# One chunk's down projection by seven products in place of eight, its sums laid into VectorE's rests

## The chip, the cores and the metric

The kernel runs on one core of a Trainium2 chip. The metric is the device time of one execution in microseconds (us), and lower is better. The profile has the engines PE (TensorE's matmuls), PEld (its weight loads), DVE (VectorE), ACT (ScalarE), POOL (GpSimd) and SP (SyncE, here only the issuer of transfers).

## The reference

A transformer layer on 2048 rows of 1024 values in bfloat16: windowed attention with an output projection, then a feed-forward part without a nonlinearity.

```python
h  = x + attention(layernorm(x), wqkv) @ wo        # wqkv 1024x3072, wo 1024x1024
g  = layernorm(h) @ w_gate                         # 1024x3584
u  = layernorm(h) @ w_up                           # 1024x3584
h2 = h + (g * u) @ w_down                          # 3584x1024
```

## The kernel before

The rows go in four chunks (0 to 3) of 512. Chunks 0 and 1 have their gate, up and down projections one chunk at a time. Chunks 2 and 3 are handled together, as a pair: their gate/up stage ("paired stage") and their down projection already use the Winograd form of Strassen's scheme, which makes a product of 2 by 2 blocks from seven block products in place of eight and pays with sums of blocks. The instruction order on each engine is the order of the program, and ScalarE and VectorE run their instructions in turn. The kernel keeps all matmul results in eight PSUM banks of 128x512, which they share.

The part that the change replaces, between chunk 1's gate/up stage and the paired stage:

```python
    hT = ffn1(1, lnT2)                 # gate and up of chunk 1, 28 tiles of hidden values
    ...
    l2, hs2 = wo_ln2(2)                # output projection of chunk 2, statistics, normalized rows
    ...
    ffn2(1, 0, hT, hs)                 # chunk 1's down projection, left half of the columns
    bg.finish(atts[3])
    l3, hs3 = wo_ln2(3)                # output projection of chunk 3
    activation_sums(l2, l3)            # the pair's sums of activations
    load_pair(0)
    load_pair(1)
    ...
    ffn2(1, 1, hT, hs, {0: first_sums})   # right half; beside it GpSimd's sums of weights

    def ffn2(c, hf, hT, hs, between={}):
        acc = [psum.tile([128, 512], F32, tag="mm", ...) for t in range(4)]
        ... # 28 tiles of hidden values x 4 blocks of rows = 112 matmuls a half
                    nc.tensor.matmul(acc[t][:], lhsT=hT[f][:, bass.ts(t, 128)],
                                     rhs=wts["wd", c, hf, b][:, j, :], ...)
        ...
        for t in range(4):
            ffn2_store(c, t, hf, acc[t], hs)   # VectorE adds the residual, then stores
```

The first step of the paired stage (`t1` to `t4` are the activation's sums, `sw` the sums of weights, `x y v z` its banks):

```python
        for i in gu:
            xb[i] = bank("x", i)
            product(xb[i], wt[:, 0:4, i, 0:128], b11, True)
            yb[i] = bank("y", i)
            nc.scalar.copy(yb[i][:], xb[i][:])
        for i in gu:
            vb[i] = bank("v", i)
            product(vb[i], sw[:, i, 0], t1, True)
            ...
            product(yb[i], sw[:, i, 1], t2, False)
            zb[i] = bank("z", i)
```

## Time and profile before

| | before |
|---|---|
| device time, median of 3 | 785.4 us (785.29 to 785.52) |
| TensorE busy | 99% |
| VectorE, ScalarE, GpSimd busy | 74%, 51%, 19% |
| end of chunk 1's gate/up to the paired stage (449.52 to 525.93) | 76.41 us |
| start of the paired stage to the end (525.93 to 785.8) | 259.9 us |

The last two rows are read off TensorE's timeline: the first matmul of chunk 2's output projection that follows the last one of chunk 1's gate/up stage, and the first `px` matmul. The stretch between them, which I call "the stage" below, begins here:

```profile
449.52 13.98 PE L507 MATMUL wo<-w_wo,oT 128*128 128x512 bf16 x63
```

It has 354 matmuls (the windows view counts 354 weight loads in it). TensorE is the bound, so the stage is read as so many matmuls at 0.216 us (112 of them took from 501.76 to 525.93) plus waits of TensorE; the busy time of the other engines matters only where one of them makes TensorE wait.

### The profile page before, as it was taken

What the parts mean: (1) busy time and instruction counts of PE and PEld (TensorE: products, weight loads), DVE (VectorE), ACT (ScalarE), POOL (GpSimd) and SP (SyncE); (2) the same over time, 40 slices, a digit from 0 to 9 for tenths busy, and PEclk for the clock granted to TensorE, in tenths of its full rate; (3) what the DMA queues carried; (4) which work ended last, traced back from release to release, by engine and by line L of the source; (5) the groups of instructions that cost most, each with busy time, mean ns of one, the idle gap of its engine ahead of it and who ended that gap; (6) DMA issues with size and microseconds to landing.
All of it is one profiled execution on the core that took longest, in us unless ns stands there. A gap on an engine that the chain in (4) does not pass through costs nothing.

```text
span 785.8 us, 10287 instructions
## 1 busy us (share of the span) xinstructions
PE 774.1 (99%) x3670; PEld 359.2 (46%) x3732; DVE 583.6 (74%) x727; ACT 402.9 (51%) x919; POOL 150.9 (19%) x160
## 2 busy tenths in 40 slices
PE   8999999999999999999999999999999999999998
PEld 6544444444444444444444444444444444444444
DVE  5619999999899998999979971733443444579862
ACT  3626534323476652965656610116677777749240
POOL 0000000010000200002000020058678687600000
PEclk9999999999999999999999999999999999999999
DMA  7999594895965878867556489433332423730001
GB/s 248 269 197 243 150 286 98 244 311 127 337 203 170 260 243 234 277 197 264 198 161 208 139 202 328 101 100 102 107 90 72 108 62 100 257 118 28 1 27 54
DMA packets 183683, 135.94 MB, mean 173 GB/s; under 512 B 79056, under 2 KB 176464, under 8 KB 181584
## 3 DMA queue, kind: packets, MB, share of 16 engines
q1 hardware_dynamic: 180048, 113.27, 51.0%
q0 software_dynamic: 3584, 22.02, 8.1%
q8 instruction: 29, 0.48, 0.3%
q14 instruction: 22, 0.18, 0.1%
HBM read 106.95 MB, written 22.02 MB: 164 GB/s over the span
## 4 chain that ended last, share of the span: by engine, by line
PE 74%; DVE 20%; issue 2%; SPq 1%; DMA 1%; ACT 0%; DVEq 0%
PE pu L386 12%; PE acc L605 12%; PE pg L386 12%; PE pz L658 6%; PE py L658 6%; PE px L658 6%; PE wo L507 5%; DVE prod L426 4%; PE ps L386 3%; PE pv L658 3%; PE dx L837 3%; PE dy L837 3%; DVE pv L469 2%; DVE prod L428 2%; SPq L223 1%
## 5 line engine op out<-in xcount | busy, mean ns | idle before, releaser
L386 PE MATMUL ps<-lnT,w_qkv 128*128 128x512 bf16 x721 | 159.0, 379 | 0.8
L386 PEld LDWEIGHTS <-w_qkv 128*128 128x128 bf16 x736 | 71.9, 98 | 86.0 <-issue 0.3
L386 PE MATMUL pu<-lnT,w_wu 128*128 128x512 bf16 x438 | 105.1, 379 | 0.6
L386 PE MATMUL pg<-lnT,w_wg 128*128 128x512 bf16 x440 | 105.1, 379 | 0.4
L605 PE MATMUL acc<-w_wd,gs 128*128 128x512 bf16 x438 | 96.7, 379 | 0.5
L300 ACT CAST sg<-ps 128x512 bf16<-128x512 f32 x96 | 54.8, 590 | 52.7 <-PE ps L386 48.9
L469 DVE TENSOR_TENSOR pv<-vD,at 128x4096 bf16<-128x4096 bf16 x32 | 72.5, 2286 | 0.3
L426 DVE TENSOR_TENSOR prod<-qD,kD 128x4096 bf16<-128x4096 bf16 x32 | 72.4, 2284 | 0.1
L658 PEld LDWEIGHTS <-sw 128*128 128x128 f16 x448 | 43.8, 98 | 52.9
L386 PEld LDWEIGHTS <-w_wg 128*128 128x128 bf16 x448 | 43.8, 98 | 52.8
L605 PEld LDWEIGHTS <-gs 128*128 128x128 bf16 x448 | 43.8, 98 | 52.9
L386 PEld LDWEIGHTS <-w_wu 128*128 128x128 bf16 x448 | 43.8, 98 | 52.9
L179 ACT ACTIVATE rs<-mv,eps 128x1 f32<-128x1 f32 x32 | 9.5, 297 | 101.2 <-DVE mv L176 98.2
L585 ACT CAST us<-pu 128x512 bf16<-128x512 f32 x56 | 33.1, 591 | 50.4 <-PE pu L386 49.3
L507 PE MATMUL wo<-w_wo,oT 128*128 128x512 bf16 x251 | 55.6, 379 | 0.3
L658 PE MATMUL px<-lnT,ws 128*128 128x512 bf16 x211 | 52.6, 379 | 0.6
L658 PEld LDWEIGHTS <-ws 128*128 128x128 f16 x336 | 32.9, 98 | 39.6
L481 POOL DMA_DIRECT2D od<-oD x4 | 2.2, 544 | 249.3 <-DVE oD L479 162.5
L637 POOL TENSOR_TENSOR sw<-ws 128x512 f16<-128x512 f16 x28 | 32.3, 1154 | 87.8 <-PE acc L605 47.2
L580 ACT CAST gs<-pg 128x512 bf16<-128x512 f32 x56 | 33.1, 591 | 12.8 <-PE pg L386 8.7
L507 PEld LDWEIGHTS <-oT 128*128 128x128 bf16 x256 | 25.0, 98 | 30.2
L428 DVE TENSOR_TENSOR prod<-prod 128x4096 bf16<-128x4096 bf16 x16 | 36.6, 2288 | 0.3
(244 smaller groups left out, 1196.6 us busy)
## 6 DMA issues: line engine op xcount, KB each, us to landing
w_wg<-in_B_w_gate_dram SPq DMA_DIRECT2D x14, 1024.0 KB, 6.7
w_wu<-in_B_w_up_dram SPq DMA_DIRECT2D x14, 1024.0 KB, 5.6
w_wd<-in_B_w_down_dram SPq DMA_DIRECT2D x16, 896.0 KB, 8.1
w_wo<-in_A_wo_dram SPq DMA_DIRECT2D x8, 1024.0 KB, 7.4
w_pair<-in_B_w_gate_dram SPq DMA_DIRECT2D x14, 512.0 KB, 4.0
w_pair<-in_B_w_up_dram SPq DMA_DIRECT2D x14, 512.0 KB, 5.3
w_qkv<-in_A_wqkv_dram SPq DMA_DIRECT2D x5, 1024.0 KB, 9.7
kd<-sg SPq DMA_DIRECT2D x32, 144.0 KB, 2.8
```

The costliest lines, as they stand in the source:

```text
L300: nc.scalar.copy(sg[:, HB:HB + TC], ps[:])
L386: nc.tensor.matmul(ps[:], lhsT=wt[:, ko, bass.ts(j, 128)], rhs=rhs[:, ko, :], start=(ko == 0), stop=(ko == KO - 1))
L426: nc.vector.tensor_tensor(prod[:, j], qD[:], kD[:, :, o:o + SUB], ALU.mult)
L428: nc.vector.tensor_tensor(prod[:, :, 0:16], prod[:, :, 0:16], prod[:, :, 16:32], ALU.add)
L469: nc.vector.tensor_tensor(pv[:, j], vD[:, :, o:o + SUB], at[:, w, None, :].to_broadcast((128, DH, SUB)), ALU.mult)
L507: nc.tensor.matmul(ps[:], lhsT=oTs[c][:, kk, t, :], rhs=wts["wo", c, hf][:, kk, :], start=(kk == 0), stop=(kk == KO - 1))
L580: nc.scalar.copy(gs[:], pg[:])
L585: nc.scalar.copy(us[:], pu[:])
L605: nc.tensor.matmul(acc[t][:], lhsT=hT[f][:, bass.ts(t, 128)], rhs=wts["wd", c, hf, b][:, j, :], start=(f == 0), stop=(f == NF - 1))
L637: nc.gpsimd.tensor_tensor(sw[:, i, 0], a21, a22, ALU.add)
L658: nc.tensor.matmul(ps[:], lhsT=lhs[:, ko, :], rhs=rhs[:, ko, :], start=(fresh and ko == 0), stop=(ko == 3), skip_group_check=not fresh)
L837: nc.tensor.matmul(ps[:, bass.ds(lo, n)], lhsT=lhs[k][:, bass.ts(q, 128)], rhs=rhs[k][:, bass.ds(lo, n)], start=(fresh and k == 0), stop=( ...
```

## The change

Chunk 1's down projection also goes by seven products. By the numbers that the prediction uses, TensorE has them in the order 1, 2, (output projection of chunk 3 after) 5, then 7, 6, 8, 9; product 1 stands ahead of chunk 2's output projection, products 2 and 5 between the two output projections, the others behind the second. Each has 28 matmuls. VectorE has to make four groups of sums of hidden values (S1 to S4, 14 sums of 256 columns each) and four sums of weights (T1 to T4), ScalarE and VectorE scale hidden values and weights from bfloat16 to float16, and the author has laid these sums between VectorE's adds of the two output projections. Beside that, a conversion of the tail moves from VectorE to ScalarE, the first sums of weights of the paired stage move from GpSimd to VectorE, the statistics of chunk 2 move from VectorE to ScalarE, one of the stage's two scale matmuls moves forward into chunk 1's gate/up stage, while one for chunk 1's hidden values comes in, and two more warming matmuls stand at the start. Cut to its core:

```diff
-    hT = ffn1(1, lnT2)
-    l2, hs2 = wo_ln2(2)
-    ffn2(1, 0, hT, hs)
-    l3, hs3 = wo_ln2(3)
-    ffn2(1, 1, hT, hs, {0: first_sums})
+    for q in range(2):
+        dprod(ex[q], q, E1["11"], fcells(dn["11"]), True)              # product 1
+    wo_adds(2, {1: scales, 2: ..., 6: lambda: t1_half(1), 7: lambda: s1(0, 10)})
+    s1(10, 14)
+    for q in range(2):
+        dprod(ex[q], q, E1["12"], fcells(dn["21"]), False)             # product 2
+        result(1, hs1[q], q, 0, ex[q], scale_d.inv, None)
...
+    for q in range(2):
+        dprod(ex[q], q, S1, fcells([dn["kx"], dn["vx"]]), True)        # product 5
+        nc.scalar.activation(p5t[:, q, :], ex[q][:], ACTF.Copy, scale=dn["inv"])
+    s3(0, 14)
+    wo_adds(3, {0: in_turn(lambda: s2(0, 7), lambda: ln_means(2)), 1: lambda: s2(7, 14),
+                2: in_turn(lambda: ln_devs(2), lambda: t2_half(0)), 3: lambda: t2_half(1), 4: lambda: t3_half(0),
+                5: in_turn(lambda: ln_act_rows(2, l2), lambda: t3_half(1)),
+                6: in_turn(lambda: ln_stats(3, 0), lambda: ln_stats(3, 1)), 7: lambda: ln_stats(3, 2)})
+    ln_stats(3, 3)                                                     # VectorE's statistics, ScalarE's root
+    for k in range(NP): ...                                            # S4, then T4
+    for q in range(2):
+        dprod(ey[q], q, EF["11"], fcells(dn["11"]), False)             # product 7
+        nc.scalar.copy(ex[q][:], ey[q][:])
+    scale_gu.total()
+    for q in range(2):
+        dprod(ex[q], q, EF["21"], fcells(dn["12"]), False)             # product 6
+        ...; result(1, hs1[2 + q], 2 + q, 1, ex[q], dn["inv"], et)
+    activation_sums(l2, l3, dn["px"])
+    weight_sums(0, nc.vector)
+    for q in range(2):
+        dprod(ex[q], q, EF["22"], fcells([dn["kx"], dn["vx"]]), False) # product 8
+        result(1, hs1[2 + q], 2 + q, 0, ex[q], dn["inv"], None)
+    for q in range(2):
+        dprod(ey[q], q, EF["12"], fcells(dn["22"]), False)             # product 9
+        result(1, hs1[q], q, 1, ey[q], dn["inv"], p5t[:, q, :])
...
-    conv_down(down["b21"])
+    conv_down(down["b21"], nc.scalar)
```

## The prediction

> **What bounds the kernel now.** I read the page's busy table first, then the waits of TensorE, then VectorE in order of time. The busy table:
>
> ```profile
> PE 774.1 (99%) x3670; PEld 359.2 (46%) x3732; DVE 583.6 (74%) x727; ACT 402.9 (51%) x919; POOL 150.9 (19%) x160
> ```
>
> TensorE is busy 99% of the span, so only fewer matmuls can pay, and every new wait of TensorE costs its full length. Busy matmuls can still be spaced out, so I looked at the issue rate. The timeline of TensorE:
>
> ```profile
> 501.76 24.34 PE L605 MATMUL acc<-w_wd,gs 128*128 128x512 bf16 x109
> 525.93 1.89 PE L658 MATMUL px<-lnT,ws 128*128 128x512 bf16 x8
> ```
>
> The second half of the down projection is 112 matmuls between 501.76 and 525.93, 0.216 us each (three records are missing). That is my unit. The waits of TensorE, and VectorE in order of time (start, us, group, idle before):
>
> ```profile
> PE dy L837 <- DVE dn_t2a L830: 1.0, 1, 1.0
> PE dy L837 <- DVE dn_t2b L830: 0.3, 1, 0.3
> ...
> 468.20 0.14 DVE L553 TENSOR_SCALAR ibd<-ebd 128x1 int32<-128x1 int32 x1
> 487.50 2.48 DVE L596 TENSOR_TENSOR h<-acc,h 128x512 bf16<-128x512 f32 x4 [19.16 <-PE acc L605]
> ...
> 525.48 2.48 DVE L596 TENSOR_TENSOR h<-acc,h 128x512 bf16<-128x512 f32 x4 [10.98 <-PE acc L605]
> ```
>
> In the part to be changed VectorE rests 19.16 us beside one half of the down projection and 10.98 us beside the other. These are the gaps in which the sums are to go. But they lie beside the very matmuls that the change cuts up, so the question is whether VectorE has each sum ready in time. The rows that I use (busy, mean ns):
>
> ```profile
> L830 DVE TENSOR_TENSOR dn_t2a<-dn_b22a,dn_t1a 128x3584 f16<-128x3584 f16 x1 | 2.0, 2007 | 0.0
> L876 DVE TENSOR_TENSOR dn_b11a<-hq,hq 128x512 f16<-128x512 f16 x6 | 2.1, 414 | 0.0
> L509 DVE TENSOR_TENSOR h<-wo,h 128x512 bf16<-128x512 f32 x32 | 21.4, 673 | 1.6 <-PE wo L507 1.6
> L784 ACT ACTIVATE dn_b22a<-dn_b22a,sbd 128x3584 f16<-128x3584 bf16 x1 | 3.3, 3283 | 0.0
> L784 ACT ACTIVATE hq<-hq,sbh 128x512 f16<-128x512 bf16 x12 | 7.6, 720 | 0.0
> ```
>
> [...]
>
> **Durations from start to start.** Sums of 3584: 1.93 (starts 730.75, 732.68, 734.62). Sums of 512: 0.334 (six in 2.08). The new sums are 256 wide, of which before has none: 0.52 ns an element between these two gives an estimate of 0.20. Scaling on VectorE: 1.07 for 3584, estimated 0.195 for 256. An add of the output projection 0.60; two statistics and their aggregate 1.44 (464.29 to 465.60, plus 0.13). VectorE starts 0.2 after a matmul group ends.
>
> **The change, part by part.**
>
> 1. Matmuls. Removed: 2 halves x 28 x 4 = 224. Added: 7 products x 2 banks x 14 = 196. Chunk 1's hidden values need their own scale: one more matmul. Net 27 x 0.216 = 5.8 us off TensorE. Without waits, from the end of chunk 1's gate/up stage to the first product of the paired stage would take 326 x 0.216 = 70.4 us in place of 76.2 (449.69 to 525.93).
>
> 2. Gate/up stage of chunk 1. ScalarE gets 28 absolute sums of 512, start to start 0.61; per pair of groups it then has 0.49 + 0.49 + 1.2 + 0.61 = 2.8 us in 3.46. It keeps up. VectorE gets two conversions (2.1 us) and is some 0.65 late from a later copy, so the last attention instruction ends at about 456 in place of 452.9. Nothing of this is on the path.
>
> 3. Output projection of chunk 2, TensorE 456.0 to 470.0 (with the one scale matmul), then product 2 to 476.0. VectorE waits for the third group (461.5) and from there is full: 6 adds 3.6, conversion of A22 2.7, of B12 2.1, T1 3.9, S1 14 x 0.20 = 2.8. Sum 15.1, so S1 is ready at 476.7; the result that frees the bank behind it takes 0.75. Product 5 starts at 477.5 in place of 476.0: **first wait 1.5 us**. It ends at 483.6.
>
> 4. Output projection of chunk 3, TensorE 483.6 to 497.4. VectorE begins with the first group's add at 485.5 and has 8 adds 4.8, S2 2.8, T2 and T3 4 x 1.93 = 7.7, four statistics 5.8, small ones 0.2: 21.3 us, to 506.9. The order list of the new kernel shows on ScalarE that the copy of product 7's banks (y to x) stands behind the four reciprocal roots of chunk 3, which need the last of these statistics. Root 0.6, copy 0.57: x is there at 508.1. TensorE has done product 7 and the other scale matmul at 503.7: **second wait 4.5 us**. Product 6 runs from 508.1 to 514.2.
>
> 5. VectorE from 506.9: the wait for the root 0.6, S4 2.8, T4 3.9, the scale chain 0.7, one add 0.7, the result of the first bank 0.75, so 516.6. Product 8 accumulates on this bank: **third wait 2.4 us**. Products 8 and 9 take 12.1, so the paired stage starts at about 528.8 in place of 525.93: 2.8 us later. Its own 12.1 us a step isn't touched; GpSimd's first sums (8 x 1.15) start at about 532 and end at 541, one step and a product later they are needed (542.6).
>
> 6. Tail. The conversion of B21 moves from VectorE (2.1) to ScalarE (6.4), which idles 7.51 us there. VectorE gets ahead by 2.1, but then one result waits for TensorE (1.1 of it lost). The waits of 1.0 and 0.3 shown above shrink by an estimated 0.75 together.
>
> 7. Start: two more warming matmuls end at 6.8, the first transpose now starts at 5.90. TensorE idles 1.03 for the weights at 7.7 and again at 9.85, which swallows the delay. I count 0.
>
> Sum: -5.8 + 1.5 + 4.5 + 2.4 + 0.2 (rounding) - 0.75 = +2.0, or 787.5.
>
> **Rivals.** (a) The order is right and TensorE never waits: 785.4 - 5.8 - 0.75 = 779. For it: the words of the change, and 37 us of rest on VectorE between 449.7 and 526. Against it: the count in 3 to 5, where each sum of durations exceeds the matmuls beside it; the rest beside chunk 0 and in the paired stage can't be used. (b) Half of it: sums of 256 are quicker than estimated or the copy reaches ScalarE earlier. If 0.05 less each, 56 sums give 2.8, but only 42 are on the path: 2.1 us, so 785.4. (c) Memory: chunk 3's attention output is fetched once chunk 2's projection is done (about 470 to 482; landing took up to 8.9 us from issue in before) for use at 483.6, and the converted B22 needs transfers issued after chunk 3's attention was stored at about 463. If they land 2 us late, 789.5. Against it: chunk 3's projection now uses chunk 2's weight blocks again, so 2 MB fewer are loaded here than before. (d) ScalarE becomes the bound in the gate/up stage by strict order: some us, 790. I give it little, 2.8 of 3.46 us is below full.
>
> **Range and chances.** My count says 787.5; the author has ordered the sums by need and will have looked at a trace, so (b) weighs more than (d). I say 786.8, with 781.5 (most of (a)) to 789.8 ((c)). For faster by 2% (769.7) more would have to go than the change removes: 1%. Slower by 2% (801) needs twice the waits that I count: 1%.
>
> **What would show it.** TensorE: 25 matmuls fewer in all (27 less, two warming ones more), and waits for VectorE ahead of product 5 (1.5), for the ScalarE copy ahead of product 6 (4.5) and for VectorE ahead of product 8 (2.4); VectorE without rest from the first add of chunk 3's projection to the statistics of its last rows; 256-wide sums at 0.27 us busy, 0.20 start to start. The step from gate/up to the paired stage should take 79 us. If it takes 71 to 74, my reading of the order or the durations of the sums are wrong; if it is right and the time isn't, the tail or the start moved.

The 0.195 us for a scaling of 256 follows from the trace of before like the 0.20 for a sum: 1.07 for 3584 and 0.263 for 512 (twelve from 706.67 to 709.82). The changed kernel has 0.196 (seven from 461.51 to 462.88).

## The result and the profile after

The changed kernel took 786.67 us (median of 4, 785.88 to 787.00), and the kernel before in the same rounds 785.46 us (785.29 to 785.55). A ratio is the mean time of one kernel's runs over that of the other's of the same rounds, so not quite the ratio of the medians; here it is 1.0014, with a 95% interval of 0.9997 to 1.0032: the same. 786.8 had been predicted.

The page of the changed kernel begins with its busy table; the columns are busy time, share of the span, number of instructions.

```profile
PE 768.9 (98%) x3648; PEld 355.4 (45%) x3707; DVE 614.6 (78%) x810; ACT 470.9 (60%) x1033; POOL 141.8 (18%) x152
```

Weight loads, of which there is one for every matmul and fewer records are missing (the down projection of chunks 0 and 1 before has 448 of them for its 448 matmuls, and 438 records of these), fell from 3732 to 3707: the 25 that were predicted. TensorE's work is 5.2 us less, VectorE's 31.0 us more, ScalarE's 68.0 us more. Where TensorE waits now (total, times, longest):

```profile
PE ex L784 <- ACT ex L963: 4.0, 1, 4.0
PE ex L784 <- DVE h L789: 2.0, 2, 1.3
...
PE dy L784 <- DVE h L789: 0.6, 1, 0.6
...
PE dy L784 <- DVE prodx L777: 0.3, 1, 0.3
```

The first two lines are new. They are the three waits of the stage (the profile counts a wait from the modelled end of the matmul before it, 0.379 us after its start, where the next one follows after 0.216 without a wait; from start to start each is 0.16 us longer: 1.48, 4.15 and 0.84); the last two are what is left of the tail's waits of 1.0, 0.6 and 0.3. The same in TensorE's timeline (start, length, group, and in brackets the wait before it and what ended it):

```profile
447.30 6.21 PE L784 MATMUL ex<-w_dn,gs 128*128 128x512 f16 x28
...
474.89 1.67 PE L784 MATMUL ex<-kx,es 128*128 128x512 f16 x7 [1.32 <-DVE h L789]
...
481.15 13.76 PE L829 MATMUL wo<-w_wo,oT 128*128 128x512 bf16 x62
...
505.16 2.09 PE L784 MATMUL ex<-w_dn,gs 128*128 128x512 f16 x7 [3.99 <-ACT ex L963]
507.05 2.98 PE L784 MATMUL ex<-prodx,gs 128*128 128x512 f16 x7
...
513.73 1.67 PE L784 MATMUL ex<-kx,gs 128*128 128x512 f16 x7 [0.68 <-DVE h L789]
...
525.81 1.89 PE L677 MATMUL px<-lnT,ws 128*128 128x512 bf16 x7
```

From top to bottom: product 1, product 5 with its wait, chunk 3's output projection, product 6 with its wait, product 8 with its wait, the paired stage. The stage takes 525.81 - 447.30 = 78.51 us. Seven matmuls of product 5 took 1.67 us in the record, seven of product 6 took 2.98: TensorE was slow there. The windows view says why (columns: window, its length, busy us of PE, PEld, DVE, ACT, POOL, the granted clock, DMA share, GB/s):

```profile
501.00:505.10 4.10, 0.17 (x1) 0.00 (x0) 3.44 (x10) 1.68 (x8) 0.00 (x0) 1.00 0.93 196
505.10:509.00 3.90, 3.84 (x12) 1.47 (x12) 3.90 (x14) 3.90 (x6) 0.00 (x0) 0.65 1.13 308
```

In the wait itself the granted clock is 1.00; in the 3.9 us behind it, 0.65. In half-microsecond windows the clock is at 0.50 from about 506.3 to 509.7, for 3.4 us. Product 6 takes 7.9 us (505.16 to 513.05) in place of the 6.2 that it takes at full clock (e4 below).

What held product 6 up, on VectorE and on ScalarE:

```profile
482.86 0.69 DVE L831 TENSOR_TENSOR h<-wo,h 128x512 bf16<-128x512 f32 x1 [4.54 <-PE wo L829]
...
503.85 0.21 DVE L182 BATCH_NORM_AGGREGATE mv<-st 128x2 f32<-128x12 f32 x1
504.66 0.16 DVE L954 SCALAR_TENSOR_TENSOR lnroom<-mv,rs 128x4 f32<-128x4 f32 x1 [0.60 <-ACT rs L186]
...
512.93 0.75 DVE L789 SCALAR_TENSOR_TENSOR h<-ex,inv_h1d,et 128x512 bf16<-128x512 f32 x1
```

```profile
504.10 0.29 ACT L185 ACTIVATE rs<-mv,eps 128x1 f32<-128x1 f32 x1 [0.86 <-DVE mv L182]
504.42 0.20 ACT L186 ACTIVATE rs<-rs 128x1 f32<-128x1 f32 x1
504.53 1.06 ACT L963 COPY ex<-ey 128x512 f32<-128x512 f32 x2
```

VectorE waits 4.54 us for chunk 3's first projection, then has no rest from 482.86 until its last statistics end at about 504.06. ScalarE makes the root of these, and only then the copy of product 7's bank, which was complete on TensorE since 501.0. The two copies take 1.06 us from 504.53; product 6 begins at 505.16, when the first of them is done. VectorE's result at 512.93 is the one that lets product 8 begin.

Two more measures. From the paired stage to the end it takes 784.8 - 525.81 = 259.0 us, 0.9 less than before. And the two profiled runs are not a fair pair: their spans are 785.8 before and 784.8 after, the other way round than the medians, because the profiled run of before had a late start, with its first 512-wide matmul at 19.38 us, against 17.08 after. Its granted clock is 0.94 in the first 30 us and at 0.50 from about 9.7 to 13.2, where that of after is 1.00. That is what the first experiment looks at.

### The profile page after: what moved, and what is told of

Read it like the earlier page. It is cut to its first block, busy times and chain, and to the rows that moved or that the text cites. A ratio compares the mean times of both kernels' runs of the same rounds, so it can differ in the third digit from the quotient of the medians.

```text
span 784.8 us, 10443 instructions
## 1 busy us (share of the span) xinstructions
PE 768.9 (98%) x3648; PEld 355.4 (45%) x3707; DVE 614.6 (78%) x810; ACT 470.9 (60%) x1033; POOL 141.8 (18%) x152
## 3 DMA queue, kind: packets, MB, share of 16 engines
q0 software_dynamic: 3584, 22.02, 8.3%
## 4 chain that ended last, share of the span: by engine, by line
PE 90%; DVE 7%; DMA 1%; issue 1%; SPq 0%; ACT 0%; DVEq 0%
PE ps L392 20%; PE pu L392 12%; PE pg L392 12%; PE dx L784 6%; PE pz L677 6%; PE py L677 6%; PE acc L626 6%; PE px L677 6%; PE wo L513 4%; PE pv L677 3%; PE dy L784 3%; PE ex L784 2%; DVE h L831 1%; PE wo L829 1%; PE ps L355 1%; DMA w_qkv<-in_A_wqkv_dram 1%
## 5 line engine op out<-in xcount | busy, mean ns | idle before, releaser
L626 PE MATMUL acc<-w_wd,gs 128*128 128x512 bf16 x219 | 48.2, 379 | 0.3
L658 POOL TENSOR_TENSOR sw<-ws 128x512 f16<-128x512 f16 x26 | 30.0, 1152 | 92.9 <-ACT pz L702 64.3
L694 ACT COPY py<-px 128x512 f32<-128x512 f32 x28 | 16.0, 570 | 35.0 <-PE px L677 35.0
L541 ACT ACTIVATE junkd<-w_wd 128x512 bf16<-128x512 bf16 x56 | 34.3, 612 | 0.0
L626 PEld LDWEIGHTS <-gs 128*128 128x128 bf16 x224 | 21.9, 98 | 26.4
```

Source lines behind the costliest of these rows:

```text
L541: nc.scalar.activation(junk, src, ACTF.Abs, accum_out=self.l1[:, k:k + 1])
L626: nc.tensor.matmul(acc[t][:], lhsT=hT[f][:, bass.ts(t, 128)], rhs=wts["wd", c, hf, b][:, j, :], start=(f == 0), stop=(f == NF - 1))
```

## The experiments

Two theories to begin with. Mine: the gain of 27 matmuls is eaten by three waits which only the order of instructions makes, and by a low clock behind the longest. The rival: the expected gain went elsewhere (a later start, the copy alone, VectorE's sheer amount of work). Runs e1 to e8 were in five rounds; e9 has four runs and e10 six. All outputs are right. The kernel before took 785.2 us (median) in the rounds of e1 to e4, 785.41 in those of e5 to e8 and 785.33 in those of e9 and e10.

### e1: only the warming

```diff
-    for i in range(11):      # in the kernel before
+    for i in range(13):
```

> The kernel before with 13 warming matmuls in place of 11, the change's edit at the start by itself. Mine: the first matmuls wait for data in any case, so the time is that of before, within 0.4 us. Rival (the two traces differ at the start: the first 512-wide product starts at 17.08 us after and 19.38 before, so the warming gives 2.3 us and hides part of the loss in the middle): 2 us or more faster than before, about 783.2.

Measured: 785.48 us (784.63 to 785.99), ratio to before 1.0002 (0.999 to 1.0015). Its first 512-wide matmul starts at 17.48 us. Its granted clock is 1.00 from 9 to 12 us and from 17 to 20, and 1.0 as the mean of the run. So two more warming matmuls change nothing in the time, and the late start of the profiled run of before is scatter, which hides in spans; stages have to be compared, or medians.

### e2: only the tail undone

```diff
-    conv_down(down["b21"], nc.scalar)     # in the changed kernel
+    conv_down(down["b21"])
```

> The changed kernel with the conversion of B21 for the last Strassen stage back on VectorE. Mine: the last stage loses what it had gained, waits of 1.0 and 0.3 us for T2 come back, so 0.7 to 0.9 us slower than the changed kernel, about 787.5. Rival (the ScalarE placement is of no use, the profile's 0.9 us from pair stage to end is noise): no difference, 786.7.

Measured: 788.04 us (787.38 to 788.38), ratio 1.0034 (1.0022 to 1.0047). The tail's wait for the sums is back, 1.3 us in place of 0.3, and from the paired stage to the end it takes 786.3 - 526.39 = 259.9 us, as in the kernel before, against 259.0 in the changed one. So that move is worth 0.9 to 1.0 us. The other 0.4 us of the difference to 786.67 is of the size of the scatter of the start (in its profiled run, which waits 1.5 us for the first weights against 0.7, the stage begins at 447.84, 0.5 us later than the changed kernel's).

### e3: only ScalarE's order

The copies of product 7's banks are put ahead of chunk 3's reciprocal roots. VectorE's and TensorE's orders stay.

```diff
     def ln_stats(c, t):
         stats(hss[c][t], mv4, t)
-        rstd_of(mv4, rs4, t, t + 1)
...
         dprod(ey[q], q, EF["11"], fcells(dn["11"]), False)
         nc.scalar.copy(ex[q][:], ey[q][:])
+    rstd_of(ln2[3][0], ln2[3][1], 0, 4)
```

> The changed kernel with only ScalarE's order altered: the two copies of product 7's banks stand ahead of chunk 3's reciprocal roots. Mine (VectorE's whole queue behind the first add of chunk 3's projection is the bound, the copy only shows it first): product 6 starts without a wait at 501.0, but product 8 still starts when VectorE has the result of its bank, at 513.7, after a wait of some 6.7 us. That wait is longer than the 4.0 us after which the clock was seen low, so product 8 runs slow for some us: time unchanged to 2 us slower, 786.7 to 788.7. Rival (the copy's place in ScalarE's queue is the loss): the wait of 4.0 us and the 1.7 us of low clock behind it go, 781 to 782.7.

Measured: 788.75 us (787.85 to 789.26), ratio 1.0043 (1.0031 to 1.0056). TensorE and the window that follows:

```profile
514.11 3.15 PE L784 MATMUL ex<-kx,gs 128*128 128x512 f16 x7 [6.52 <-DVE h L789]
```

```profile
514.00:518.00 4.00, 3.89 (x10) 1.38 (x10) 2.84 (x5) 0.00 (x0) 0.00 (x0) 0.53 0.70 159
```

Product 6 now starts without a wait, so ScalarE's strict turn did cause the wait of 4.0 us. But nothing is gained: product 8 waits 6.52 us for VectorE's result. The clock falls within this wait, at an estimated 511.0 (it is 0.72 on average from 509.0 to 513.5 and 0.50 from 511.0 to 514.0), and is 0.53 behind it; here no later wait hides that, and the stage takes 80.31 us, 1.8 more than the changed kernel's. The copy was the visible wait, and VectorE's list behind it set the end.

### e4: the wait filled with useless matmuls

```diff
-    scale_gu.total()
+    scale_gu.total(again=19)     # 18 more matmuls of the same sum, which change nothing
```

> The changed kernel with 18 more matmuls of no use (the scale sum again) in the 4.0 us wait ahead of product 6, so that TensorE does not rest there. Mine: product 6 then runs at the full clock, 6.05 us in place of 7.9, but the wait ahead of product 8 grows from 0.7 to 2.4 us, the value that I predicted, since VectorE sets when product 8 starts: time unchanged within 0.4 us. Rival (the low clock after a wait is a loss of its own): 1.7 us faster, about 785.0.

Measured: 787.57 us (787.0 to 788.84), ratio 1.0033 (1.0019 to 1.0047). TensorE and the window that showed 0.65 in the changed kernel:

```profile
514.71 1.67 PE L785 MATMUL ex<-kx,gs 128*128 128x512 f16 x7 [2.37 <-DVE h L790]
```

```profile
505.10:509.00 3.90, 3.83 (x19) 1.64 (x18) 3.36 (x16) 3.87 (x7) 0.00 (x0) 1.00 1.14 311
```

The clock stays full (1.00 from 501.0 to 518.0), product 6 takes 6.2 us, and product 8's wait becomes 2.37 us, in place of 0.68. The stage takes 78.52 us, as long as the changed kernel's 78.51. So the low clock cost nothing there: it ran inside a wait that would have been there anyway. The whole time is 0.9 us above the changed kernel's with an equal stage; that lies before the stage, which begins at 448.27 in place of 447.30 (from the paired stage to the end it is 259.0 us in both), and I have no cause for it beyond the scatter of the start.

### e5: the changed kernel again

> The changed kernel once more, unchanged, so that the other three kernels of this call have it beside them on the same chip. I expect a median of about 786.7 us and a ratio to the kernel before of 1.001 to 1.002, and in its profile the three waits of the paired stage as they were: about 1.3 us ahead of product 5, 4.0 us ahead of product 6 (for ScalarE's copy) and 0.7 us ahead of product 8, with a stretch of lowered TensorE clock after the 4.0 us wait, and a stage of about 78.5 us. If instead the stage varied by more than half a microsecond from run to run, the readings of the other kernels against it would be worth less.

Measured: 786.67 us (785.97 to 786.87), ratio 1.0015 (1.0001 to 1.0028). Waits of 1.32 and 4.00 us, and none ahead of product 8, for product 6 took 8.7 us here (505.09 to 513.80) and so swallowed all of it; stage 525.89 - 447.21 = 78.68. The stage repeats within 0.2 us. The low clock does not repeat: here it is at 0.50 from 505.00 to 509.00, so already when product 6 begins, and its mean of 0.68 from 508.00 to 512.00 puts its end at an estimated 510.6. That is an estimated 5.5 us or more, in place of 3.4.

### e6: the second group of sums in VectorE's rest

```diff
     s3(0, 14)
-    wo_adds(3, {0: in_turn(lambda: s2(0, 7), lambda: ln_means(2)), 1: lambda: s2(7, 14),
-                2: in_turn(lambda: ln_devs(2), lambda: t2_half(0)), 3: lambda: t2_half(1), 4: lambda: t3_half(0),
-                5: in_turn(lambda: ln_act_rows(2, l2), lambda: t3_half(1)),
+    s2(0, 14)
+    wo_adds(3, {0: in_turn(lambda: t2_half(0), lambda: ln_means(2)), 1: lambda: t2_half(1),
+                2: in_turn(lambda: ln_devs(2), lambda: t3_half(0)), 3: lambda: t3_half(1),
+                5: lambda: ln_act_rows(2, l2),
```

> The changed kernel with only VectorE's order changed: the 14 sums of the second group are made in the 4.5 us in which VectorE waits for chunk 3's first output projection, and the shares of the third and fourth group move one place forward in the adds of chunk 3. My theory says that chunk 3's last statistics, and with them ScalarE's roots and its copy, wait for a VectorE that has too much to do after that 4.5 us rest. Moving 14 x 0.20 = 2.8 us of work into the rest should then end the statistics about 2.6 us earlier: the wait of product 6 falls from 4.0 to about 1.4 us, TensorE's clock stays full there, the wait of product 8 becomes about 2.5 us (it no longer hides in a low clock), the stage takes about 75.9 us and the kernel about 2.6 us less than the changed one, some 784.1 us. The rival says that the last product waits for the results in any case, because VectorE's work behind the statistics is what counts: then the wait only moves from product 6 to product 8 and the time stays at 786 to 787 us.

Measured: 785.72 us (785.53 to 785.89), ratio 1.0005 (0.9992 to 1.0018). TensorE's timeline:

```profile
502.87 1.67 PE L784 MATMUL ex<-w_dn,gs 128*128 128x512 f16 x7 [1.31 <-ACT ex L964]
...
511.43 1.67 PE L784 MATMUL ex<-kx,gs 128*128 128x512 f16 x7 [2.36 <-DVE h L789]
...
525.86 1.02 PE L677 MATMUL pv<-prodx,sw 128*128 128x512 f16 x4 [0.45 <-DVE h L789]
```

Inside the stage everything is as the theory had it: 1.31 and 2.36 us, the clock full (1.00 from 501.0 to 518.0), the stage 523.51 - 447.68 = 75.83 us. But only about 1 us of the 2.7 arrives at the end (785.72 against 786.67), and I had expected all of it: from the paired stage to the end it takes 260.6 us in place of 259.0, with new waits of 0.45 and 0.64 us at its start. VectorE shows where they come from:

```profile
512.21 0.75 DVE L789 SCALAR_TENSOR_TENSOR h<-ex,inv_h1d,et 128x512 bf16<-128x512 f32 x1
516.13 1.23 DVE L669 TENSOR_TENSOR prodx<-lnT,lnT 128x2048 f16<-128x2048 bf16 x1 [3.17 <-DMA lnT<-lnr]
```

VectorE waits 3.17 us for the transposed rows of chunk 3, which its next sums read, and behind these sums stand the results that free the banks of the paired stage.

### e7: the result ahead of the first group's sums

```diff
-                6: lambda: t1_half(1), 7: lambda: s1(0, 10)})
-    s1(10, 14)
+                6: lambda: t1_half(1)})
...
         dprod(ex[q], q, E1["12"], fcells(dn["21"]), False)
+        if q == 1:
+            s1(0, 14)
         result(1, hs1[q], q, 0, ex[q], scale_d.inv, None)
```

> The changed kernel with the result that frees product 5's bank put ahead of the 14 sums of the first group on VectorE, and nothing else moved. My prediction said that product 5 waits 1.5 us (1.3 measured) because VectorE makes those sums first. The theory expects that wait to go to 0 and everything behind it on TensorE, the first output projection of chunk 3 included, to come 1.3 us earlier, and as VectorE waits for that projection, the statistics come 1.3 us earlier too: waits of product 6 and 8 as before (4.0 and 0.7), the stage 77.2 us, the kernel about 785.4 us. The rival says that VectorE's own work is the chain, so that the 1.3 us come back as a longer wait of product 6 (5.3 us) and the time stays at 786.7 us.

Measured: 785.41 us (785.34 to 786.18), ratio 1.0003 (0.9991 to 1.0016). Product 5 starts without a wait, directly behind product 2, which began at 467.54:

```profile
473.58 1.67 PE L784 MATMUL ex<-kx,es 128*128 128x512 f16 x7
```

Product 6 waits 4.00 us as before, and the stage takes 524.55 - 447.46 = 77.09 us, 1.4 less. The theory's numbers, and not the rival's 5.3 us. The time is 1.26 us less than e5's by the medians and 0.9 by the means of five.

### e8: the whole stage in order of need

The edits of e3, e6 and e7 together, and these (product 9's results also go ahead of product 8's):

```diff
+    scale_gu.total()                      # the scaling chain in VectorE's rest
...
     for q in range(2):
         dprod(ex[q], q, EF["21"], fcells(dn["12"]), False)
+    for q in range(2):
+        dprod(ey[q], q, EF["12"], fcells(dn["22"]), False)   # product 9 ahead of product 8
+    weight_sums(0)                        # on GpSimd again, not on VectorE
     for q in range(2):                    # product 6's results only now
         nc.vector.tensor_tensor(et[:], p5t[:, q, :], hs1[2 + q][:, 512:1024], ALU.add)
         result(1, hs1[2 + q], 2 + q, 1, ex[q], dn["inv"], et)
```

> All in one, in an order of need: the result ahead of the first group's sums, the second group's sums and the scaling chain of the next stage in VectorE's 4.5 us rest, the third and fourth group earlier, ScalarE's copies ahead of chunk 3's roots, product 9 ahead of product 8, the last group's sums ahead of the results, and one of the sums of weights back on GpSimd. If the three waits of the paired stage are a matter of order alone, as my theory has it, none is left: the stage takes its matmuls' 326 x 0.216 us, about 70.6 us, in place of 78.5 us, and the kernel 778.6 to 779.5 us, less than both kernels by 6 to 8 us (ratio to the kernel before 0.992). The rival says that VectorE has too much to do in this stage whatever the order, and that one of the displaced works (the statistics of chunk 3, the activation's sums, GpSimd's sum) is then late for the next stage: some 3 to 4 us of waits remain, at another product or in the next stage, and the time is 782 us or more.

Measured: 785.63 us (784.39 to 786.23), ratio 1.0003 (0.999 to 1.0015). The stage is what I expected, 518.33 - 447.97 = 70.36 us without any wait of TensorE, and the time is not. TensorE's next wait:

```profile
524.98 1.86 PE L677 MATMUL pv<-prodx,sw 128*128 128x512 f16 x4 [4.76 <-DVE h L789]
```

and VectorE up to it:

```profile
515.07 2.13 DVE L669 TENSOR_TENSOR prodx<-lnT,lnT 128x2048 f16<-128x2048 bf16 x1 [2.45 <-DMA lnT<-lnr]
517.23 2.06 DVE L670 TENSOR_TENSOR prodx<-lnT,prodx 128x2048 f16<-128x2048 bf16 x1
519.21 2.17 DVE L671 TENSOR_TENSOR prodx<-lnT 128x2048 f16<-128x2048 bf16 x1
521.30 2.17 DVE L672 TENSOR_TENSOR prodx<-lnT,prodx 128x2048 f16<-128x2048 bf16 x1
...
524.18 0.75 DVE L789 SCALAR_TENSOR_TENSOR h<-ey,inv_h1d,ep 128x512 bf16<-128x512 f32 x1
```

As in e6, the activation's four sums wait for the transposed rows, and product 9's result stands behind them, although its two banks were complete at 509.3 and 512.3. The earlier TensorE reaches the paired stage, the more of this list becomes a wait. Two more things came on top. GpSimd is now at work beside these sums, and they take 2.06 to 2.17 us in place of 1.22 in the changed kernel, 3.6 us in all. GpSimd's own sums take up to 2.13 us beside them, against 1.15 while VectorE rested. Both are longer where the two engines work at once; no run takes one of the two away to show why. And the clock behind the wait falls to 0.52 (525.0 to 528.3). From the paired stage to the end it takes 265.5 us in place of 259.0. So this time the rival was right: a displaced work was late for the next stage.

### e9 and e10: the results ahead of the activation's sums

e9 is e8 with the two results of product 9 ahead of the four sums, and the two of product 8 behind the first and the second of them. e10 moves only product 9's.

```diff
-    activation_sums(l2, l3, dn["px"])
     for q in range(2):
         dprod(ex[q], q, EF["22"], fcells([dn["kx"], dn["vx"]]), False)
     for q in range(2):
         nc.vector.tensor_tensor(p5t[:, q, :], p5t[:, q, :], hs1[q][:, 512:1024], ALU.add)
         result(1, hs1[q], q, 1, ey[q], dn["inv"], p5t[:, q, :])
-    for q in range(2):
-        result(1, hs1[2 + q], 2 + q, 0, ex[q], dn["inv"], None)
+    activation_sums(l2, l3, dn["px"], [        # e9: one result after each of the first two sums
+        lambda q=q: result(1, hs1[2 + q], 2 + q, 0, ex[q], dn["inv"], None) for q in range(2)])
```

> The kernel in order of need (the last one), with the results of chunk 1 no longer behind the activation's sums on VectorE: the two results of product 9 ahead of them, the two of product 8 after the first and the second of the four sums. In the last kernel the stage was the expected 70.4 us, but then the paired stage's third bank waited 4.8 us for these results, which stood behind sums that wait until 515.1 us for the transposed rows of chunk 3. My theory: VectorE rests in that wait, so the results fit in there, the sums end no more than 3 us later and in time for their products, and the wait of 4.8 us and the low clock behind it (1.6 us) go away: the stage 70.4 us, the paired stage and the tail 259 us, the time 779 us (778.3 to 780.0), ratio to the kernel before 0.992. The rival says that the transposed rows of chunk 3 are too late for the paired stage in themselves: then its wait only moves to the first or second sum and the time stays at 783 us or above.

Measured, e9: **778.43 us** (777.91 to 778.66), ratio to before 0.991 (0.9895 to 0.9926). This beats both kernels, by 6.9 us the one before. TensorE goes from product 8 into the paired stage without a wait:

```profile
517.71 1.89 PE L679 MATMUL px<-lnT,ws 128*128 128x512 bf16 x7
519.44 1.03 PE L679 MATMUL pv<-prodx,sw 128*128 128x512 f16 x4
```

The stage is 517.71 - 447.35 = 70.36 us, the rest 776.7 - 517.71 = 259.0 us, and the mean granted clock 1.000. On VectorE the results fill what was a wait for the transfer:

```profile
514.38 0.75 DVE L791 SCALAR_TENSOR_TENSOR h<-ey,inv_h1d,ep 128x512 bf16<-128x512 f32 x1
515.05 1.32 DVE L669 TENSOR_TENSOR prodx<-lnT,lnT 128x2048 f16<-128x2048 bf16 x1
```

The first sum starts at 515.05 and no longer waits; the rows are there. TensorE's records of that run show no wait over 0.6 us behind the start.

> As the run above, but only product 9's two results ahead of the activation's sums; product 8's two results stay behind all four. If it is the results that free the paired stage's banks in order (theory), the third and fourth pair of banks of its first step now wait for product 8's results: the sums end at about 523.4 us by the clock of the last kernel's trace and the first of these results at about 524.1, while TensorE would want the bank at about 521.8 to 523.5: a wait of some 1 to 2.5 us in the first step and a time of 780 to 781.5 us. If the wait had to do with the transposed rows alone (rival), both kernels of this call take the same time.

Measured, e10: 781.63 us (780.46 to 782.8), ratio 0.995 (0.9937 to 0.9964). One wait is back:

```profile
523.54 1.02 PE L677 MATMUL pv<-prodx,sw 128*128 128x512 f16 x4 [2.03 <-DVE h L789]
```

It is the second `pv` bank that waits, and 2.0 us lie within the 1 to 2.5 that I had expected; the median is 0.1 above what I had. But it stands for neither half of the runs: three took 780.5 to 780.7 us at a mean granted clock of 0.999 to 1.000, three, the profiled one among them, 782.6 to 782.8 at 0.997 to 0.998. So the wait alone costs some 2.1 us against e9, and the runs with the lower mean clock took 2.2 us more, of which 3.4 us at half the clock make 1.7. In the 2.0 us of the wait the granted clock of the profiled run is 1.00, from 525.5 to 527.5 it is 0.50. So the rows are in time, and the results that free the banks are what e8 waited for.

## Why the prediction was right, step by step

1. **Matmuls.** 27 fewer, 70.4 us without waits: e8 and e9 measure 70.36. Right, and shown by a run rather than counted. Two details were off: 449.69 is the modelled end of the last gate/up matmul, while the next one starts at 449.52, so the stage before is 76.41 us, not 76.24; and the stage loses 28 matmuls (354 to 326), since one scale matmul moved into the gate/up stage.
2. **Gate/up stage.** ScalarE was to need 2.8 of 3.46 us a pair of groups. The trace has it idle for 0.74 of 3.45, so 2.7 busy, and TensorE has no wait there. Rival (d) falls.
3. **First wait.** 1.5 predicted, 1.32 measured (1.48 from start to start, as the prediction counts), and e7 shows the cause: with the result ahead of the sums it is gone, and about 1 us of it arrives in the time.
4. **Second wait.** 4.5 predicted (its 508.1 and 503.7 make 4.4), 3.99 measured, 4.15 from start to start. The mechanism, the copy in turn behind the roots, is shown by e3 and VectorE's list before them by e6. In VectorE's 21.3 us the 256-wide sums were right at 0.20 us from start to start (14 in 2.8 us); their busy time is 0.28 where 0.27 was said. From the stage's start to the end of the last statistics it is 56.8 us (447.30 to 504.06), where I had 57.2 (449.69 to 506.9).
5. **Third wait.** 2.4 predicted, 0.68 measured. This is the mis-sized term. It was computed from product 6 at full clock; the wait of 4 us was followed by a low clock, product 6 took 7.89 where e4's took 6.20, and those 1.69 us lie in the place of the wait. 0.68 + 1.69 = 2.37, and e4, which keeps the clock up, measures 2.37 as a wait. The end of the stage was nearly right, the name of the loss was not. The 2.4 had luck in it too: the durations listed in the prediction's step 5 add up to 516.35, not 516.6, and give 2.15. Low clock was in none of my steps.
6. **Tail.** -0.75 predicted, -0.9 measured, and the wait undone in e2 is 1.0.
7. **Start.** 0 predicted; e1 agrees.

The stage was to be 2.8 us longer and is 2.1 (78.51 against 76.41). From start to start, and with the low clock counted to the third wait, the measured terms are -6.05 + 1.48 + 4.15 + 2.53 = +2.11. With the tail's -0.9 that makes +1.2 us, and the medians differ by 1.2. The count in the text said +2.0, or 787.5, and I took off 0.7 for rival (b), quicker sums or an earlier copy. The sums were not quicker; what the count had too much was one matmul in the stage, 0.2 of rounding and some 0.3 in the second wait. So the mechanism was right, and that 786.8 came within 0.2 us of the median was luck. Rival (a), no waits, 779, named the time of another kernel: e9 has 778.43. Rival (c), memory, had no wait of TensorE within the stage in any of these runs. Another transfer, the transposed rows of chunk 3, shows as a wait of VectorE: 1.12 us in the changed kernel, 3.17 in e6, 2.45 in e8.

What the prediction did not see is what is behind the three waits. Shortening the second (e6) or removing all together (e8) uncovered a fourth at the next stage's banks, which the changed kernel hides in its own lateness; removing the first alone (e7) did not yet. e8 lost 6.5 us to this of the 8.2 that its stage had won, and two places in VectorE's list gave it back.

How much of e8's 4.8 us would stay if GpSimd had been silent beside the sums is not settled: the 3.6 us are a difference of durations between two kernels, and no run took GpSimd's part alone away. Taken as they are, they would leave an estimated 4.8 - 3.6 = 1.2 us. Nor does any run say which of e8's edits e9 could do without.

## What to carry to other kernels

A scheme that saves matmuls and pays with sums is worth what the order of the sums leaves of it: here nearly the same sums gave -6.9 us in one order and +1.2 in another. An in-order engine's list has to be read for instructions that wait for a transfer, since whatever frees a bank belongs ahead of them (in e8 a wait of 2.45 us for a transfer stands in the list behind which TensorE waited 4.76 us). When a wait is removed and the time does not follow, look at the first wait of the next stage before doubting the theory, and compare stages rather than spans.

## What the runs show of the clock behind a wait

- The runs show no length of a wait from which on the clock falls. A wait of 2.03 us was followed by a clock of 0.50 in the profiled run of e10, while waits of 2.36 and 2.37 us were not (e6 with 1.00 from 511.4 to 514.4, e4 with 1.00 from 514.0 to 518.0). So a wait of 2 us can cost, and a somewhat longer one need not; three of e10's six runs kept a mean clock of 0.999 to 1.000. In e10 the clock did not fall in the wait but about 1 us after the matmuls had begun again: 1.00 from 523.5 to 524.5, 0.62 in the next microsecond. In e7 the first seven matmuls behind the wait of 4.00 us took 3.15 us, where seven take 1.67 at full clock, so there it was low from the first of them. In windows of a microsecond or less the low stretch adds up to 3.4 us in the changed kernel, e8 and e10. In e5 it is an estimated 5.5 us or more, and in e7 5.1 us or more: the first 14 matmuls of product 6 took 5.58 us (503.86 to 509.44) in place of 14 x 0.216 = 3.02, and at half the clock 5.1 us lose those 2.56.
